# Forty-four of 1024 softmax score tiles take their exponential on VectorE and GpSimd instead of ScalarE

## The chip, the core and the metric

The kernel runs as one program on one core of a Trainium2 chip. The metric is device time in microseconds (us) of one execution. The kernel before was timed in three runs: 493.62, 494.31 and 499.47 us, median 494.31 us. One further execution was profiled; it took 492.96 us, and the span that the profile shows of it is 491.2 us.

Names of engines as in the profile: PE is TensorE, DVE is VectorE, ACT is ScalarE, POOL is GpSimd, SP issues DMAs. PSUM is the memory that PE writes to, in banks of 512 float32 per partition; SBUF is the working memory.

## The reference

The input is 2048 tokens of 448 numbers. Branch A is attention with 16 heads of 28, branch B a filter in the frequency domain; a sigmoid gate per token mixes them.

```
g = sigmoid((x * gate_w).sum(-1))
q, k, v = split(x @ wqkv)                 # 16 heads of 28
p = softmax(q @ k.T * 28 ** -0.5)         # 2048 x 2048 for each head
a = (p @ v) merged @ wo
b = irfft2(rfft2(x) * (w_r + 1j * w_i))
out = g * a + (1 - g) * b
```

The softmax has 16 x 2048 x 2048 = 67 million scores, and each needs an exponential. This is what the change is about.

## The kernel before, in words

**Tiles.** The scores are kept transposed: a score tile is 128 keys by 512 queries of one head, so one PSUM bank. Heads go in four groups T of four heads (`s` = 0 to 3, each on 32 rows of PE); queries go in four quarters q. A pair (T, q) is a chunk, and there are 16 chunks of 16 key blocks `i` by 4 heads, so 64 tiles each, 1024 in all.

**Steps.** `attention` (L554) cuts the row of 1024 tiles into steps of three (L558). Each step is one buffer `psS` of three PSUM banks, of which there are two (L158), and one exponential on ACT over all three banks, 128 x 1536, written as bf16 to `Pt` (`exps`, L582; six buffers `Pt`). That makes 341 ACT instructions of three tiles and one of one tile. The scale 28 ** -0.5 is given to it as an immediate, and so is a bias of zero. The queries were shifted beforehand by half norms (`nhk`), so that no maximum is needed.

**Order within step m** (L611 to L626): ACT's exponential of step m; PE's three score matmuls of step m+1 (`scores`, L565), with filler matmuls on a zero tile `warm` ahead of them where a count of PE's work says so (`filler`, L490); PE's value matmuls of eight finished tiles at a time (`values`, L591) into one PSUM bank `psPV`; then other work (`other_work`, L501); then whatever was put down in `later[m]`. A helper class (L113) keeps this order on every engine's queue: an engine runs its instructions in the order in which they were written, and one that waits holds up those behind it.

**Values.** `vsb` has a column of ones, so the sums of the softmax come out in `psPV` too. With a chunk's last tile, `normalise` (L671) puts down for later steps: a DVE transpose of `psPV` to `oU`, a reciprocal on DVE, a multiplication on POOL (`on`), and a DVE transpose to `oT` (which is `qT`). There is one `psPV` (L161), so the next chunk's first value matmul needs that first transpose done.

**Other work** is a list of units with due steps (`plan`, L438): keys and queries of later head groups (`k_units`, `q_units`), values, and the whole of branch B in matmuls (names `X`, `U`, `UT`, `Xri`, `G`, `V`, `VT`, `ZT`, `bm`). A unit is some PE matmuls into the one PSUM bank `bg` (L164), and then a DVE instruction that brings the bank to SBUF; the next unit can't write `bg` before. The budget of a step is `ROOM` = 1.22 us of PE time by a count of columns. POOL squares keys and queries (`sq`) for the half norms, multiplies in `normalise`, and does half of the complex product (`cm_t`, `G`).

**Ends.** `finish` (L629) does the last chunk's output. Before the first exponential, `head` (L243) transposes x and makes the first keys and queries. In it ACT runs some instructions with a bias read from SBUF (`keep`, L280, L284: `kT<-pk,kbt`) and some without (`sq<-pk`, L278).

Of the kernel before, what the change touches and what calls it, by code (L numbers as in the profile page):

```python
# [8 lines left out]

BF16 = mybir.dt.bfloat16  # L10
F32 = mybir.dt.float32
ACT = mybir.ActivationFunctionType
ALU = mybir.AluOpType
AX = mybir.AxisListType

P = 128
# [19 lines left out]
FEND = 318  # L36
BUSY = 1650
UNIT = 1000
F = D // 2 + 1
F2 = 2 * F  # L40
J = P // NT
# [94 lines left out]
class Kernel:  # L136
# [42 lines left out]
    def loads(self):  # L179
        nc, per = self.nc, self.per  # L180
        cc = self.consts = fft_consts()
        self.warm = per.tile([P, QW], BF16, name="warm")
        nc.vector.memset(self.warm[:], 0.0)
        c_IS = nc.inline_tensor(cc["IS"], name="cIS")
        self.IS = per.tile([P, 2 * P], BF16, name="IS")
        wqkv = self.A_wqkv.rearrange("(c p) (w n) -> p c w n", p=CK, w=3)
        self.W0 = per.tile([CK, NC_, 2, CK], BF16, name="W0")
        nc.sync.dma_start(out=self.W0[:, :, 1, :], in_=wqkv[:, :, 1, 0:CK])
        nc.scalar.dma_start(out=self.IS[:], in_=c_IS.ap())
        nc.scalar.dma_start(out=self.W0[:, :, 0, :], in_=wqkv[:, :, 0, 0:CK])  # L190
        self.ident = self.IS[:, 0:P]
        self.sel = self.IS[:, P:2 * P]
        self.xtok = [per.tile([P, 4, D], BF16, name=f"xtok{g}", tag=f"xb{g}") for g in range(4)]
        for g in range(4):
            nc.sync.dma_start(out=self.xtok[g][:], in_=self.x[:, 4 * g:4 * g + 4, :])
        self.kbt = per.tile([P, 1], F32, name="kbt")
        self.kb = self.kbt[:, 0:1]
        wv = self.A_wqkv[:, 2 * D:3 * D].rearrange("(c p) n -> p c n", p=CK)
        self.Wv = per.tile([CK, NC_, D + 1], BF16, name="Wv")
        nc.sync.dma_start(out=self.Wv[:, :, 1:D + 1], in_=wv)  # L200
        nc.sync.dma_start(out=self.Wv[:, :, 0:1],
                          in_=self.gate_w.rearrange("(c p o) -> p c o", p=CK, o=1))
        self.Wqk = per.tile([CK, NC_, 2 * D], BF16, name="Wqk")
        nc.sync.dma_start(out=self.Wqk[:],
                          in_=self.A_wqkv[:, 0:2 * D].rearrange("(c p) n -> p c n", p=CK))
        self.Bd = per.tile([CK, NC_, F2], BF16, name="Bd")
        nc.sync.dma_start(out=self.Bd[:], in_=nc.inline_tensor(cc["Bd"], name="cBd").ap())
        self.WqP = per.tile([CK, NC_, H, 32], BF16, name="WqP")
        self.WkP = per.tile([CK, NC_, H, 32], BF16, name="WkP")
        for Wp in (self.WkP, self.WqP):  # L210
            nc.gpsimd.memset(Wp[:, :, :, DH:32], 0.0)
        self.vsb = per.tile([P, NT, H, 32], BF16, name="vsb")
        nc.gpsimd.memset(self.vsb[:, :, :, DH:32], 0.0)
        nc.gpsimd.memset(self.vsb[:, :, :, DH:DH + 1], 1.0)
        self.wk = self.Wqk[:, :, D:2 * D].rearrange("p c (h d) -> p c h d", d=DH)
        self.wq = self.Wqk[:, :, 0:D].rearrange("p c (h d) -> p c h d", d=DH)
        self.xT = per.tile([CK, NC_, S], BF16, name="xT")
        self.qT = [per.tile([P, S], BF16, name=f"qT{T}") for T in range(NTH)]
        self.kT = [per.tile([P, S], BF16, name=f"kT{T}") for T in range(NTH)]
        self.oT = self.qT  # L220
        self.nm = [per.tile([P, NQ], F32, name=f"nm{T}") for T in range(NTH)]
        self.nhk = [per.tile([P, 1], F32, name=f"nhk{T}") for T in range(NTH)]
        self.glog = per.tile([P, NT], F32, name="glog")
        self.gsb = per.tile([P, NT], F32, name="gsb")
        self.omg = per.tile([P, NT], F32, name="omg")
        self.R = per.tile([P, 4, 256], BF16, name="R")
        self.Binv = per.tile([P, 2 * len(FCH), D], BF16, name="Binv")
        self.c_CS = nc.inline_tensor(cc["CS"], name="cCS")
        self.c_RB = nc.inline_tensor(cc["RB"], name="cRB")
        self.Wr_v = self.B_w_r.rearrange("(m g) f -> g m f", g=NT)  # L230
        self.Wi_v = self.B_w_i.rearrange("(m g) f -> g m f", g=NT)
        self.WoP = per.tile([P, NTH, D], BF16, name="WoP")
        nc.gpsimd.memset(self.WoP[:], 0.0)
# [128 lines left out]
    def q_units(self, T, g):  # L362
# [17 lines left out]
                                           op0=ALU.add, op1=ALU.add)  # L380
        return (("qa", T, g), a), (("q", T, g), b)

    def k_units(self, T, g):
        nc = self.nc
        st = {}

        def a():
            pk = self.ps_bg([P, QW], F32, name="pkb")
            yield from self.proj_mm(pk[:], self.WkP, T, g)
            kT = self.kT[T][:, QW * g:QW * g + QW]  # L390
            nc.vector.tensor_scalar(out=kT, in0=pk[:], scalar1=self.kb, scalar2=None,
                                    op0=ALU.add)
            sq = st["sq"] = self.rot3.tile([P, QW], BF16, name="sq")
            nc.gpsimd.tensor_tensor(out=sq[:], in0=kT, in1=kT, op=ALU.mult)
# [150 lines left out]
    def gate(self):  # L545
# [5 lines left out]
        nc.vector.tensor_scalar(out=self.omg[:], in0=self.gsb[:], scalar1=-1.0, scalar2=1.0,  # L551
                                op0=ALU.mult, op1=ALU.add)

    def attention(self):  # L554
        nc = self.nc
        chunks = [(T, q) for T in range(NTH) for q in range(NQ)]
        seq = [(ci, i, s) for ci in range(len(chunks)) for i in range(NT) for s in range(4)]
        steps = [seq[m:m + 3] for m in range(0, len(seq), 3)]  # L558
        n = len(steps)
        psS, Pt = {}, {}  # L560

        group = [len([1 for k in range(3 * m, 3 * m + 3) if k % GROUP == GROUP - 1])
                 for m in range(n + 1)]

        def scores(m):  # L565
            T, q = chunks[steps[m][-1][0]]
            self.need(("k", T, NQ - 1))
            self.need(("q", T, q))
            ps = psS[m] = self.ps_S([P, 3, QW], F32, name="psS")
            self.base = QW  # L570
            if m > 1:
                pv = GROUP // 4 * QW * group[m - 2]
                room = ROOM + ALLOW - self.over - 3 * SWITCH - QW * MM - pv * MM
                self.base += self.filler(m - 1, room, QW + pv, ps)
            for e, (ci, i, s) in enumerate(steps[m]):
                T, q = chunks[ci]
                nc.tensor.matmul(ps[:, e, :],
                                 lhsT=self.kT[T][32 * s:32 * s + 32, P * i:P * i + P],
                                 rhs=self.qT[T][32 * s:32 * s + 32, QW * q:QW * q + QW],
                                 start=True, stop=True, tile_position=(32 * s, 0))  # L580

        def exps(m):  # L582
            ne = len(steps[m])
            pt = Pt[m] = self.rotP.tile([P, 3, QW], BF16, name="Pt")
            nc.scalar.activation(out=pt[:, 0:ne, :], in_=psS.pop(m)[:, 0:ne, :], func=ACT.Exp,
                                 scale=SCALE)

        self.psPV = None
        pending = []

        def values(m, least):  # L591
            room = 0.0
            while len(pending) >= least:
                ci = pending[0][2][0]
                T, q = chunks[ci]
                for pt, e, (_, i, s) in pending[:least]:
                    self.need(("v", 1, i) if T else ("v", 0, i // 2))
                    if i == 0 and s == 0:
                        self.psPV = self.ps_pv([P, QW], F32, name="psPV")
                    nc.tensor.matmul(self.psPV[32 * s:32 * s + 32, :],  # L600
                                     lhsT=self.vsb[:, i, 4 * T + s, :], rhs=pt[:, e, :],
                                     start=(i == 0), stop=(i == NT - 1), tile_position=(0, 32 * s))
                del pending[:least]
                room += SWITCH + least / 4 * QW * MM
                self.base += least // 4 * QW
                if i == NT - 1 and s == 3:
                    self.normalise(m, T, q, self.psPV)
            return room

        scores(0)  # L610
        for m in range(n + 1):  # L611
            if m < n:
                exps(m)
            if m + 1 < n:
                scores(m + 1)
            if m > 0:
                pending += [(Pt[m - 1], e, x) for e, x in enumerate(steps[m - 1])]
            late = m >= n - 3
            fill = self.base - QW
            used = fill * MM + values(m, 4 if late else GROUP)  # L620
            used += 2 * SWITCH + QW * MM
            if m < n:
                used += self.other_work(m, ROOM + ALLOW - self.over - used, self.base)
            self.over = max(0.0, self.over + used - ROOM)
            for f in self.later.pop(m, []):
                f()  # L626
        assert not (self.current or self.units or self.later)
# [298 lines left out]
```

## Time and profile before

| what | value |
|---|---|
| three runs | 493.62, 494.31, 499.47 us; median 494.31 |
| the profiled execution | 492.96 us, span 491.2 us, mean granted PE clock 0.986 |
| busy: PE, DVE, ACT, POOL | 392.2, 195.5, 471.3, 85.5 us |
| first exponential starts, last three-tile one ends | 18.31 us, 480.73 us |
| DMA | 12.67 MB, mean 26 GB/s |

A row of the list of groups reads: line, engine, operation, written<-read, shapes, number of instructions, then busy time in us and mean ns of one, then the idle time of the engine just before them and what ended it. Nearly all rows have line L119, since a helper records every instruction; the names of the tiles tell them apart. Busy time is a union: where records of one engine overlap, the time is counted once, while the mean is of the whole records. A row of the timeline is start, length, engine, operation, tiles, shape and count, with the idle time before it in brackets; one row can hold several instructions in a row, and its length then runs from the first start to the last end. In the table of stretches, each row gives the length of the stretch and then each engine's busy time and number of instructions.

### The profile page before, as it was taken

To read this page: it belongs to the slowest core of one execution; us is meant where nothing else is said; L and a number is where in the kernel's file an instruction comes from. 1 tells how busy PE (TensorE), PEld (TensorE's weight loads), DVE (VectorE), ACT (ScalarE), POOL (GpSimd) and SP (SyncE) were. 2 spreads that over 40 slices of the span, in tenths; PEclk is the share of its full clock that TensorE was granted. 3 is DMA by queue.
4 is the path that set the end of the run, shared out by engine and by line. 5 is a ranking of instruction groups with operands and counts; after the bars stand their busy time and mean duration, and the time that the engine had idled before them with its cause. 6 is when DMAs were issued, how large, how long until landed. Compare 5 with 4: busy or idle time off the path is not lost.

```text
span 491.2 us, 7735 instructions
## 1 busy us (share of the span) xinstructions
PE 392.2 (80%) x3154; PEld 146.4 (30%) x3154; DVE 195.5 (40%) x338; ACT 471.3 (96%) x364; POOL 85.5 (17%) x125
## 2 busy tenths in 40 slices
PE   8877777779878887877777778778887778888876
PEld 5422222222222233332333223333233232323221
DVE  5421222322332344437566664443333333434413
ACT  5899999999999999998999999999999999999992
POOL 4100111040000111105455541101000000000000
PEclk9999999998999999998999999999999999999997
DMA  8800000000000000001122200000000000100001
GB/s 253 194 1 1 2 1 0 1 0 1 1 1 1 0 1 1 0 2 43 39 62 53 67 1 0 2 1 21 12 23 11 23 12 20 52 29 20 11 28 38
DMA packets 15515, 12.67 MB, mean 26 GB/s; under 512 B 6984, under 2 KB 14600, under 8 KB 15480
## 3 DMA queue, kind: packets, MB, share of 16 engines
q1 hardware_dynamic: 14728, 11.91, 9.0%
q8 instruction: 24, 0.39, 0.3%
q10 hardware_dynamic: 752, 0.28, 0.2%
q14 instruction: 11, 0.09, 0.1%
HBM read 10.35 MB, written 1.84 MB: 25 GB/s over the span
## 4 chain that ended last, share of the span: by engine, by line
ACT 57%; issue 21%; PE 16%; DVE 3%; DMA 1%; POOL 1%; DVEq 0%; SPq 0%; ACTq 0%; POOLq 0%
ACT Pt L119 57%; PE psS L119 5%; PE psPV L119 3%; PE pq L119 1%; PE pvp L119 1%; DMA xtok<-in_A_x_dram 1%; PE pt L119 1%; PE pwt L119 1%; PE pk L119 1%; PE psB L119 1%; DVE qT L119 0%; PE pkb L119 0%; DVE kT L119 0%; DVE qr L119 0%; POOL sq L119 0%
## 5 line engine op out<-in xcount | busy, mean ns | idle before, releaser
L119 ACT ACTIVATE Pt<-psS 128x1536 bf16<-128x1536 f32 x342 | 459.9, 1613 | 4.8 <-PE psS L119 4.6
L119 PE MATMUL psS<-qT,kT 32*128 32x512 bf16 x1024 | 134.8, 385 | 44.9 <-ACT Pt L119 41.6
L119 PEld LDWEIGHTS <-kT 32*128 32x128 bf16 x1024 | 42.5, 91 | 160.5 <-issue 156.2
L119 PE MATMUL psPV<-Pt,vsb 128*32 128x512 bf16 x1024 | 80.5, 390 | 1.2 <-DVE oU L119 1.2
L119 PE MATMUL psS<-warm 128*128 128x512 bf16 (+14 forms) x152 | 41.8, 332 | 21.4 <-ACT Pt L119 20.6
L119 POOL TENSOR_TENSOR sq<-qr 128x512 bf16<-128x512 bf16 x16 | 16.7, 1041 | 134.4 <-DVE qr L119 134.4
L119 POOL TENSOR_TENSOR sq<-kT 128x512 bf16<-128x512 bf16 x12 | 12.5, 1041 | 114.9 <-DVE kT L119 114.9
L119 POOL TENSOR_TENSOR on<-oU,rc 128x512 bf16<-128x512 f32 x15 | 15.7, 1048 | 90.5 <-DVE rc L119 90.5
L119 PEld LDWEIGHTS <-warm 128*128 128x128 bf16 x178 | 17.4, 101 | 36.6 <-issue 31.9
L119 POOL TENSOR_TENSOR cm_t<-Xri,Wg 128x225 bf16<-128x225 bf16 x32 | 20.3, 655 | 29.0 <-DVE Xri L119 29.0
L119 PEld LDWEIGHTS <-vsb 128*32 128x32 bf16 x1024 | 15.6, 94 | 30.9 <-issue 30.9
L119 DVE CAST vsb<-pvp 128x336 bf16<-128x336 f32 x16 | 8.1, 508 | 36.3 <-PE pvp L119 36.3
L119 DVE CAST X<-psx 128x450 bf16<-128x450 f32 x16 | 10.0, 627 | 30.4 <-PE psx L119 30.4
L119 DVE TENSOR_SCALAR bm<-psY,omg 128x448 bf16<-128x448 f32 x16 | 10.9, 684 | 24.4 <-PE psY L119 24.4
L119 DVE CAST qr<-pq 128x512 bf16<-128x512 f32 x16 | 11.1, 691 | 23.9 <-PE pq L119 23.9
L119 PEld LDWEIGHTS <-xT 112*128 112x128 bf16 x192 | 13.4, 97 | 22.2 <-issue 18.1
L119 PE MATMUL pq<-xT,WqP 112*128 112x512 bf16 x64 | 18.1, 381 | 1.8 <-DVE U L119 0.5
L119 DVE CAST ZT<-psZ 113x512 bf16<-113x512 f32 x16 | 11.1, 692 | 17.2 <-PE psZ L119 17.2
L119 PE MATMUL pf<-WoP,qT 128*128 128x448 bf16 x60 | 15.7, 355 | 2.2 <-DVE qT L119 0.8
L119 PE MATMUL psx<-Bd,xT 112*128 112x450 bf16 x64 | 16.5, 357 | 1.0 <-DVE kT L119 0.5
L119 DVE CAST U<-psA 113x512 bf16<-113x512 f32 x16 | 11.1, 692 | 15.3 <-PE psA L119 15.3
L119 DVE SCALAR_TENSOR_TENSOR fin<-pf,gsb,bm 128x448 bf16<-128x448 f32 x12 | 8.2, 684 | 21.7 <-PE pf L119 21.7
(82 smaller groups left out, 350.2 us busy)
## 6 DMA issues: line engine op xcount, KB each, us to landing
RBg<-cRB SPq DMA_DIRECT2D x16, 128.0 KB, 2.1
xtok<-in_A_x_dram SPq DMA_DIRECT2D x4, 448.0 KB, 4.7
out_dram<-fin SPq DMA_DIRECT2D x15, 112.0 KB, 1.7
CSg<-cCS SPq DMA_DIRECT2D x16, 96.0 KB, 1.9
Wg<-in_B_w_r_dram SPq DMA_DIRECT2D x16, 56.2 KB, 1.8
Wg<-in_B_w_i_dram SPq DMA_DIRECT2D x16, 56.2 KB, 1.9
Wqk<-in_A_wqkv_dram SPq DMA_DIRECT2D x1, 784.0 KB, 10.4
Binv<-cBinv SPq DMA_DIRECT2D x1, 448.0 KB, 13.7
```

The costliest lines, as they stand in the source:

```text
L119: return lambda *a, **k: self._tc.keep_in_program_order(f(*a, **k))
```

## The change

A few tiles of each chunk leave ACT. `AWAY` says at which steps after a chunk's start one tile is taken away: 0, 5 and 11 in fourteen chunks, 0 alone in chunks 7 and 8, so 44 tiles. Such a step still has three score tiles in its three banks, but ACT's exponential covers two of them, 128 x 1024. So ACT now has 297 exponentials of three tiles, 44 of two and one of one: 342, as before.

The third bank is read by DVE. With y = score * scale / ln 2 * 2^23 taken as an integer, the upper bits are the exponent of the result and the lower 23 a fraction; the result is the power of two times a polynomial of degree four in the fraction. Per tile (128 x 512) there are

- on DVE: `bits` from PSUM (multiply, maximum, to int32), in step m; `frac` (and, or) in step m+1; the power of two (and, xor, in place in `bits`) in m+2; three instructions `scalar_tensor_tensor` on float32 in m+5, m+6 and m+7, the last of which writes bf16 `px`;
- on POOL: an addition of a constant and a multiplication, both float32, in m+1.

The value matmul of such a tile comes `LAG` = 9 steps after its score. The leading coefficient is not multiplied in: instead every exponential on ACT now has a bias, log(2 / POLY[4]), read from a tile `shift` (128 x 1 in SBUF), where before the bias was an immediate zero. The budget of a step with a tile taken away is 0.4 us smaller (`SHORT`).

`kT` of groups 2 and 3 now takes the buffers of groups 0 and 1, and `Wqk` shares a buffer with `U` and `V` (tag `UV`). No DMA is added or moved. PE has the same 1024 score and 1024 value matmuls, and 158 fillers in `psS` instead of 152.

```
+BITS = SCALE / float(np.log(2.0)) * 2.0 ** 23
+LEAST = -126.0 * 2.0 ** 23
+ONE = 0x3F800000
+POLY = (37.67976179, 23.05395003, 12.31057451, -0.15702562, 0.01353417)
+AWAY = {c: [0, 5, 11] if c not in (7, 8) else [0] for c in range(16)}
+LAG = 9
+SHORT = 0.4
...
+        self.shift = per.tile([P, 1], F32, name="shift")
+        nc.vector.memset(self.shift[:], float(np.log(2.0 / POLY[4])))
...
-        self.Wqk = per.tile([CK, NC_, 2 * D], BF16, name="Wqk")
+        self.Wqk = per.tile([CK, NC_, 2 * D], BF16, name="Wqk", tag="UV")
...
+    def new_keys(self, T):
+        self.kT[T] = self.per.tile([P, S], BF16, name=f"kT{T}", tag=f"kT{T % 2}")
...
+    def away(self, m, score, turn):
+        nc = self.nc
+        bits = self.rot2.tile([P, QW], I32, name="bits")
+        frac = self.rot2.tile([P, QW], I32, name="frac")
+        h = self.rot2.tile([P, QW], F32, name="horner")
+        px = self.rot3.tile([P, QW], BF16, name="px")
+        read = nc.vector.tensor_scalar(out=bits[:], in0=score, scalar1=BITS, scalar2=LEAST,
+                                       op0=ALU.mult, op1=ALU.max)
...
+        def fraction():
+            nc.vector.tensor_scalar(out=frac[:], in0=bits[:], scalar1=0x7FFFFF, scalar2=ONE,
+                                    op0=ALU.bitwise_and, op1=ALU.bitwise_or)
+            nc.gpsimd.tensor_scalar(out=h[:], in0=x, scalar1=POLY[3], scalar2=None, op0=ALU.add)
+            nc.gpsimd.tensor_tensor(out=h[:], in0=h[:], in1=x, op=ALU.mult)
+
+        def power():
+            nc.vector.tensor_scalar(out=bits[:], in0=bits[:], scalar1=0x7F800000,
+                                    scalar2=0x40000000, op0=ALU.bitwise_and,
+                                    op1=ALU.bitwise_xor)
+
+        def times(c, by, out):
+            nc.vector.scalar_tensor_tensor(out=out[:], in0=h[:], scalar=c, in1=by,
+                                           op0=ALU.add, op1=ALU.mult)
+        for d, f in ((1, fraction), (2, power), (5, lambda: times(POLY[2], x, h)),
+                     (6, lambda: times(POLY[1], x, h)),
+                     (7, lambda: times(POLY[0], bits[:].bitcast(F32), px))):
+            self.later.setdefault(m + d, []).append(f)
+        return px
...
         def exps(m):
-            ne = len(steps[m])
-            pt = Pt[m] = self.rotP.tile([P, 3, QW], BF16, name="Pt")
-            nc.scalar.activation(out=pt[:, 0:ne, :], in_=psS.pop(m)[:, 0:ne, :], func=ACT.Exp,
-                                 scale=SCALE)
+            acts, away = steps[m]
+            ne = len(acts)
+            ps = psS.pop(m)
+            pt = self.rotP.tile([P, 3, QW], BF16, name="Pt")
+            turn = nc.scalar.activation(out=pt[:, 0:ne, :], in_=ps[:, 0:ne, :], func=ACT.Exp,
+                                        scale=SCALE, bias=self.shift[:, 0:1])
+            ready.setdefault(m + 1, []).extend((pt[:, e, :], x) for e, x in enumerate(acts))
+            for x in away:
+                px = self.away(m, ps[:, ne, :], turn)
+                ready.setdefault(m + LAG, []).append((px[:], x))
...
+            self.room = ROOM
             if m < n:
+                self.room -= SHORT * len(steps[m][1])
                 exps(m)
```

More of the change, by code (lines that the diff above doesn't have):

```diff
@@ L11 @@
 F32 = mybir.dt.float32
+I32 = mybir.dt.int32
 ACT = mybir.ActivationFunctionType
@@ L218, in loads @@
         self.qT = [per.tile([P, S], BF16, name=f"qT{T}") for T in range(NTH)]
-        self.kT = [per.tile([P, S], BF16, name=f"kT{T}") for T in range(NTH)]
+        self.kT = {}
+        self.new_keys(0)
         self.oT = self.qT
@@ L387, in a @@
         def a():
+            if g == 0:
+                self.new_keys(T)
             pk = self.ps_bg([P, QW], F32, name="pkb")
@@ L552, in gate, with steps @@
                                 op0=ALU.mult, op1=ALU.add)
+    def steps(self, chunks):
+        away, acts = {}, []
+        for ci in range(len(chunks)):
+            away[ci] = [(o, (ci, 4 * k, k)) for k, o in enumerate(AWAY.get(ci, []))]
+            out = [x for _, x in away[ci]]
+            acts += [(ci, i, s) for i in range(NT) for s in range(4) if (ci, i, s) not in out]
+        steps, first = [], {}
+        while acts:
+            ci = acts[0][0]
+            m = len(steps)
+            first.setdefault(ci, m)
+            off = [away[ci].pop(0)[1]] if away[ci] and away[ci][0][0] <= m - first[ci] else []
+            k = 3 - len(off)
+            steps.append((acts[:k], off))
+            del acts[:k]
+        assert not any(away.values())
+        return steps
@@ new lines, in away @@
+    def away(self, m, score, turn):
[6 more added lines that the diff above has]
+                                       op0=ALU.mult, op1=ALU.max)
+        self.tc.declare_no_dep(read.ins, turn.ins, reason="another bank")
+        x = frac[:].bitcast(F32)
+        def fraction():
[15 more added lines that the diff above has]
+        return px
@@ L556, in attention @@
         chunks = [(T, q) for T in range(NTH) for q in range(NQ)]
-        seq = [(ci, i, s) for ci in range(len(chunks)) for i in range(NT) for s in range(4)]
-        steps = [seq[m:m + 3] for m in range(0, len(seq), 3)]
+        steps = self.steps(chunks)
         n = len(steps)
-        psS, Pt = {}, {}
-        group = [len([1 for k in range(3 * m, 3 * m + 3) if k % GROUP == GROUP - 1])
-                 for m in range(n + 1)]
+        psS, ready = {}, {}
+        ends = [0]
+        for m in range(n + 1):
+            new = len(steps[m - 1][0]) if m else 0
+            new += sum(1 for k in (m - LAG,) if k >= 0 and steps[k][1])
+            ends.append(ends[-1] + new)
+        group = [ends[m + 1] // GROUP - ends[m] // GROUP for m in range(n + 1)]
         def scores(m):
-            T, q = chunks[steps[m][-1][0]]
+            tiles = steps[m][0] + steps[m][1]
+            T, q = chunks[tiles[len(steps[m][0]) - 1][0]]
             self.need(("k", T, NQ - 1))
@@ L571, in scores @@
             if m > 1:
-                pv = GROUP // 4 * QW * group[m - 2]
-                room = ROOM + ALLOW - self.over - 3 * SWITCH - QW * MM - pv * MM
+                pv = GROUP // 4 * QW * group[m - 1]
+                room = self.room + ALLOW - self.over - 3 * SWITCH - QW * MM - pv * MM
                 self.base += self.filler(m - 1, room, QW + pv, ps)
-            for e, (ci, i, s) in enumerate(steps[m]):
+            for e, (ci, i, s) in enumerate(tiles):
                 T, q = chunks[ci]
@@ L582, in exps @@
         def exps(m):
-            ne = len(steps[m])
-            pt = Pt[m] = self.rotP.tile([P, 3, QW], BF16, name="Pt")
-            nc.scalar.activation(out=pt[:, 0:ne, :], in_=psS.pop(m)[:, 0:ne, :], func=ACT.Exp,
-                                 scale=SCALE)
+            acts, away = steps[m]
[8 more added lines that the diff above has]
+                ready.setdefault(m + LAG, []).append((px[:], x))
         self.psPV = None
         pending = []
+        count = [0] * 4
         def values(m, least):
@@ L593, in values @@
             while len(pending) >= least:
-                ci = pending[0][2][0]
-                T, q = chunks[ci]
-                for pt, e, (_, i, s) in pending[:least]:
+                for ap, (ci, i, s) in pending[:least]:
+                    T, q = chunks[ci]
                     self.need(("v", 1, i) if T else ("v", 0, i // 2))
-                    if i == 0 and s == 0:
+                    if not any(count):
                         self.psPV = self.ps_pv([P, QW], F32, name="psPV")
                     nc.tensor.matmul(self.psPV[32 * s:32 * s + 32, :],
-                                     lhsT=self.vsb[:, i, 4 * T + s, :], rhs=pt[:, e, :],
-                                     start=(i == 0), stop=(i == NT - 1), tile_position=(0, 32 * s))
+                                     lhsT=self.vsb[:, i, 4 * T + s, :], rhs=ap,
+                                     start=(count[s] == 0), stop=(count[s] == NT - 1),
+                                     tile_position=(0, 32 * s))
+                    count[s] += 1
                 del pending[:least]
@@ L605, in values @@
                 self.base += least // 4 * QW
-                if i == NT - 1 and s == 3:
+                if min(count) == NT:
+                    count[:] = [0] * 4
                     self.normalise(m, T, q, self.psPV)
             return room
+        self.room = ROOM
         scores(0)
         for m in range(n + 1):
+            self.room = ROOM
             if m < n:
+                self.room -= SHORT * len(steps[m][1])
                 exps(m)
@@ L615, in attention @@
                 scores(m + 1)
-            if m > 0:
-                pending += [(Pt[m - 1], e, x) for e, x in enumerate(steps[m - 1])]
+            pending += ready.pop(m, [])
             late = m >= n - 3
@@ L622, in attention @@
             if m < n:
-                used += self.other_work(m, ROOM + ALLOW - self.over - used, self.base)
-            self.over = max(0.0, self.over + used - ROOM)
+                used += self.other_work(m, self.room + ALLOW - self.over - used, self.base)
+            self.over = max(0.0, self.over + used - self.room)
             for f in self.later.pop(m, []):
```

## The prediction

> **What bounds the kernel now.** I read the page first for who is busy, then the groups, then the timeline of ACT in the head for the one thing that the change does to every exponential, then a stall, then a table of stretches.
>
> The page: ACT is busy 96% of the span, and the chain that ended last lies on its exponentials.
>
> ```profile
> span 491.2 us, 7735 instructions
> PE 392.2 (80%) x3154; PEld 146.4 (30%) x3154; DVE 195.5 (40%) x338; ACT 471.3 (96%) x364; POOL 85.5 (17%) x125
> ...
> ACT 57%; issue 21%; PE 16%; DVE 3%; DMA 1%; POOL 1%; DVEq 0%; SPq 0%; ACTq 0%; POOLq 0%
> ```
>
> The groups. The 342 exponentials make 459.9 us of the 491.2, with only 4.8 us of idle time before them: ACT sets the time. Their records overlap (342 x 1613 ns would be 552 us), so the price of one is not 1613 ns but busy time over count: the first starts at 18.31 us and the 341st ends at 480.73, so 462.4 us less 4.8 idle, over 341, is 1.342 us. The other rows give prices for the added work.
>
> ```profile
> L119 ACT ACTIVATE Pt<-psS 128x1536 bf16<-128x1536 f32 x342 | 459.9, 1613 | 4.8 <-PE psS L119 4.6
> ...
> L119 POOL TENSOR_TENSOR on<-oU,rc 128x512 bf16<-128x512 f32 x15 | 15.7, 1048 | 90.5 <-DVE rc L119 90.5
> ...
> L119 DVE SCALAR_TENSOR_TENSOR qT<-pq,nhk,qr 128x512 bf16<-128x512 f32 x15 | 11.2, 749 | 10.7 <-PE pq L119 10.7
> ...
> L119 DVE TENSOR_SCALAR kT<-pkb,kbt 128x512 bf16<-128x512 f32 x12 | 9.0, 747 | 16.2 <-PE pkb L119 16.2
> ...
> L119 ACT ACTIVATE sq<-pk 128x512 bf16<-128x512 f32 x4 | 2.4, 600 | 1.3 <-PE pk L119 1.3
> ...
> L119 ACT ACTIVATE kT<-pk,kbt 128x512 bf16<-128x512 f32 x3 | 1.9, 685 | 0.0
> ```
>
> ACT's timeline at the end gives the price per element: 128x1536 alone takes 1.45 us, 128x512 alone 0.60 us, so 1024 elements are 0.85 us and one tile is 0.427 us.
>
> ```profile
> 479.28 1.45 ACT L119 ACTIVATE Pt<-psS 128x1536 bf16<-128x1536 f32 x1
> 481.38 0.60 ACT L119 ACTIVATE Pt<-psS 128x512 bf16<-128x512 f32 x1 [0.65 <-PE psS L119]
> ```
>
> ACT's timeline in the head shows what a bias read from SBUF costs. `sq` has an immediate bias, `kT` a bias from the tile `kbt`; both read 128x512 from PSUM.
>
> ```profile
> 11.77 0.60 ACT L119 ACTIVATE sq<-pk 128x512 bf16<-128x512 f32 x1 [0.94 <-PE pk L119]
> 12.27 0.68 ACT L119 ACTIVATE kT<-pk,kbt 128x512 bf16<-128x512 f32 x1
> 12.84 1.01 ACT L119 COPY xT<-pt 112x1024 bf16<-112x1024 bf16 x1
> ...
> 14.68 0.60 ACT L119 ACTIVATE sq<-pk 128x512 bf16<-128x512 f32 x1 [0.33 <-PE pk L119]
> 15.17 1.26 ACT L119 ACTIVATE kT<-pk,kbt 128x512 bf16<-128x512 f32 x2
> ```
>
> From `sq` to the next start is 0.50 us (11.77 to 12.27) and 0.49 (14.68 to 15.17). From `kT` to the next start is 0.57 (12.27 to 12.84), and two `kT` back to back last 1.26 us, which is 0.68 and a pitch of 0.58. No idle time lies between them. So the bias from SBUF adds 0.07 to 0.09 us to what an instruction holds the engine, even where the next one is already there.
>
> A stall, and the load of DVE by stretch:
>
> ```profile
> 224.89 0.70 DVE L119 STREAM_TRANSPOSE oU<-psPV 128x512 f32<-128x512 f32 x1
> ...
> 225.65 0.83 PE L119 MATMUL psPV<-Pt,vsb 128*32 128x512 bf16 x8 [1.18 <-DVE oU L119]
> ...
> 227.55 1.45 ACT L119 ACTIVATE Pt<-psS 128x1536 bf16<-128x1536 f32 x1 [0.84 <-PE psS L119]
> ```
>
> ```profile
> 220.00:249.00 29.00, 22.63 (x197) 8.73 (x197) 18.18 (x36) 27.52 (x21) 13.37 (x20) 0.94 0.17 41
> 249.00:278.00 29.00, 21.77 (x208) 8.77 (x208) 19.21 (x37) 29.00 (x23) 15.21 (x23) 1.00 0.28 69
> 278.00:336.00 58.00, 45.99 (x382) 18.92 (x380) 28.84 (x46) 57.38 (x44) 13.80 (x17) 1.00 0.01 2
> ```
>
> The stall shows how DVE, which bounds nothing, reaches ACT: DVE came late to the transpose of `psPV`, PE waited 1.18 us, and ACT then 0.84 us for scores. But DVE at 66% (249 to 278: 19.21 of 29.00) stalls ACT not at all.
>
> **The change, part by part.**
>
> *Fewer elements on ACT.* 44 tiles x 0.427 us = -18.8 us, all on the path. The number of exponentials stays 342, so no fixed cost goes.
>
> *A bias from SBUF in every exponential.* The trace has no exponential with one; it has `kT`. Bounds: 0, if it hides behind the overlap of the long records, and 0.09 us, from the two `kT` back to back (0.58 less 0.49). I take 0.076, from the unrounded starts of those same rows (494 and 570 ns), since `kT` held its successor up by it with no idle time between. 341 x 0.076 = +25.9 us (0 to +30.7). A rule speaks on this: the Trainium skill, "ScalarE: Activation LUTs", section "What ACT_TABLE_LOAD costs", says that each pointer operand of one value per partition adds about 93 ns to an instruction, beside 186 ns and 0.833 ns per element, and that neighbours overlap by about 93 ns. By that figure the term would be 341 x 0.093 = +31.7 us, an estimate from that page, and the change slower still; the rows decide, and I keep theirs.
>
> These two give +7.1 us for a stream of exponentials that never waits.
>
> *The score buffer is held by DVE too.* Scores of step m+2 need both ACT's exponential and DVE's `bits` of step m done. A two-tile exponential takes 1.342 + 0.076 - 0.427 = 0.99 us from the end of the one before. `bits` costs 0.75 (the row of `kT` on DVE, also 128x512 from PSUM). It is queued on DVE behind whatever brought `bg` home for step m-1, and in 14 of the 44 places behind a polynomial instruction of the tile before. With DVE free it ends 0.8 after the exponential's start, so nothing is lost; behind a full 0.75 us instruction it ends at 1.56, 0.57 late. Behind the wait on PE stand value matmuls and other work, and ACT two steps on. Scores took 0.39 us and were ready a median 0.59 us before ACT needed them (their ends against the ends of the exponentials), which covers most of it. Bounds: 0 to 44 x 0.57 = 25 us; I take +1.5, nearer to nothing because of that lead.
>
> *The polynomial on DVE and POOL.* On DVE 0.75 for `bits`, 3 x 0.75 (row `qT<-pq`), and two bit operations between 0.24 (the reciprocal on 16 elements, a fixed cost) and 0.75: I take 0.5, together 4.0 us a tile, 176 us in all. DVE goes from 195.5 to 371 us, some 74%. On POOL two operations of at most 1.05 (row `on`): 92 us on top of 85.5. No element of that is on the path by itself: of the nine steps to the value matmul, seven are taken, and the 2.1 us on POOL have four steps (5.6 us). For the bit operations, which read float-sized integers in SBUF, "VectorE: DVE Perf Modes", "The perf-mode tier table", gives two elements a cycle; with that page's 58 cycles of fixed cost and 0.96 GHz it would be 0.33 us each, an estimate from the page that no row here shows, and DVE's load some 15 us smaller.
>
> What it costs is that evacuations come later. From 278 to 336 six tiles bring DVE from 28.84 to 53 us of 58; from 220 to 278 only two are added, 78%. There `psPV`'s transpose and `bg` wait longer, and PE with them. Against that, 297 steps are 76 ns longer, which is PE's to spend. Bounds: -4 us, if the longer steps remove nearly all of the 4.8 us of idle time, and +12, if each stretch of 29 us stalls like 220 to 249 (1.5 us for half of the 16 chunks). I take +3.
>
> *At nothing:* squares `sq` and `on` get up to 2.1 us of POOL ahead of them; POOL is 17% busy, and the matmul that needs `sq` comes a unit later (if that cover went, 27 x 1 us). `kT` of groups 2 and 3 is first written at 166.7 and 283.7 us, and its new buffer was last read when chunks 3 and 7 ended, about 133 and 250 us. `U` is written from 176 us on, `Wqk` was last copied at 103 us. SP's and POOL's DMA queues are not touched. The memset of `shift` is one small DVE instruction in the head. Six more fillers: PE waits for ACT anyway. Tail (480.7 to 491.2) and head (18.3) stay.
>
> Sum: -18.8 + 25.9 + 1.5 + 3 = +11.6 us. On the profiled execution (492.96, span 491.2) that is 504.6, span 502.8; the median of the runs lies 1.35 above that execution, and against it 494.31 + 11.6 = 505.9. I say 505.5.
>
> **The rivals.**
>
> 1. *The bias hides* (faster). Exponentials are dispatched while the one before is still in flight: mean record 1.61 for a pitch of 1.34, so 0.27 us ahead, three times what the bias costs. If it is fetched in that time, the term is 0: 494.31 - 18.8 + 4.5 = 480. Break-even is 18.8 / 341 = 55 ns per exponential, 42 ns with the waits. Against it: `kT` was followed without a gap too, overlapped its successor by 0.11 us, and still held it by the full 0.076.
> 2. *The bias costs, and the waits do not come* (within 2%). The longer steps give PE more room, DVE's added load is off the path: 494.31 + 7.1 - 2 = 499. For it: the stretch at 66% DVE without a stall.
> 3. *DVE becomes the local bound* (slower by far). DVE at 91% from 278 to 336, and `bits` holding the score buffers in all places: +7.1 and 12 to 25 of stalls, 513 to 526, say 520. Against it: 74% on the whole, and nine steps of patience.
>
> **How the numbers follow.** Chances: forecast (bias in full, stalls of 3 to 12 us) 0.55, 501.5 to 512; rival 1 0.08; rival 2 0.22, 495 to 501.5; rival 3 0.15. The range takes rival 2 whole and the lower part of rival 3: 495 to 517. Slower by over 2%, which is about what a measurement of this kernel can tell from no change, is above 504.2: 0.37 of the forecast's 0.55 and rival 3, 0.52. Within 2%: the rest of the forecast and rival 2, 0.40. Faster by over 2%: 0.08.
>
> **What would show it.** In the profile after, three-tile exponentials at a pitch of 1.42 us confirm the bias, at 1.34 refute it; two-tile ones at 0.99 or 0.92. ACT's idle time before `Pt` should be 8 to 12 us; over 15 is rival 3. `bits<-psS` near 0.75 us, DVE busy near 371 us, and waits of `psS` for DVE `bits` few and short. It is wrong if the bias is free, or if DVE's queue makes PE wait at most of the 44 places.

## The result, and the profile after

The changed kernel took 541.0 us in the median of four runs (536.4 to 547.4); the kernel before 494.4. The ratio is 1.089, with a 95% interval of 1.077 to 1.101; it is one of means and leaves out the run of 547.4 us, which fell in a slower state, while the medians here and below are of all runs. The profiled execution took 539.06 us, its span is 537.3 us (491.2 before).

The page of the changed kernel: its first line, the busy times, and the chain of waits. ACT is still the busiest, but in a longer span, and PE, DVE and POOL now hold 61% of the chain, where it was 20%.

```profile
span 537.3 us, 8096 instructions
PE 423.2 (79%) x3160; PEld 150.6 (28%) x3160; DVE 350.1 (65%) x603; ACT 488.4 (91%) x364; POOL 218.0 (41%) x213
...
PE 30%; ACT 26%; DVE 22%; issue 13%; POOL 9%; DVEq 0%; ACTq 0%; POOLq 0%
```

The groups of the changed kernel: the exponential, and POOL's two operations for a tile taken away. The idle time before the exponentials went from 4.8 us to 34.7. POOL needs 1.52 and 1.32 us, where the prediction had at most 1.05 each.

```profile
L127 ACT ACTIVATE Pt<-psS,shift 128x1536 bf16<-128x1536 f32 (+1 forms) x342 | 477.0, 1508 | 34.7 <-PE psS L127 33.9
...
L127 POOL TENSOR_SCALAR horner<-frac 128x512 f32<-128x512 f32 x44 | 66.9, 1521 | 193.7 <-DVE frac L127 193.7
...
L127 POOL TENSOR_TENSOR horner<-horner,frac 128x512 f32<-128x512 f32 x44 | 57.9, 1315 | 3.7
```

ACT's timeline in a stretch without waits gives the new pitch: seven exponentials in 10.14 us, one of them alone 1.54, so (10.14 - 1.54) / 6 = 1.433 us.

```profile
336.26 10.14 ACT L127 ACTIVATE Pt<-psS,shift 128x1536 bf16<-128x1536 f32 x7
```

The list of waits of the changed kernel (who waited for whom: us in all, times, longest):

```profile
PEld L127 <- DVE bits L127: 42.7, 39, 3.9
ACT Pt L127 <- PE psS L127: 33.9, 41, 4.0
...
PE psS L127 <- DVE bits L127: 21.5, 20, 3.7
...
DVE qT L127 <- POOL on L127: 20.1, 13, 3.7
```

PE's weight loads wait for `bits` 39 times; there are 44 such places. And DVE waits 20.1 us for POOL's `on`. The same line of the kernel before:

```profile
DVE qT L119 <- POOL on L119: 4.8, 4, 2.0
```

To add the waits up for every kernel in the same way, I take from each trace the ends of successive exponentials. Their distance in undisturbed steps is the pitch of the form, and its sum over all steps is the "stream"; what is longer than the pitch is "waits". (The idle time in the row above is a little smaller, because an exponential that starts late has no record in front of it to overlap with.) Before: pitch 1.342, stream 456.3, waits 4.7. After: pitch 1.431 and 1.004, stream 468.2, waits 40.8. So 11.9 us of the 46 came from the stream and 36.1 from waits; a rest of some -2 us lies at the first and last exponential and in the tail. Every stream and every wait below is read from one profiled execution of its kernel, while the times of one kernel spread by up to 11 us, so differences of a few us are not firm.

**Where the waits come from.** The timeline of the changed kernel around step 5 of chunk 1 shows the main case (chunks and their steps count from 0). The rows of PE's weight loads and some others are left out.

```profile
52.60 5.49 ACT L127 ACTIVATE Pt<-psS,shift 128x1536 bf16<-128x1536 f32 x4
...
53.68 1.66 POOL L127 TENSOR_SCALAR horner<-frac 128x512 f32<-128x512 f32 x1
...
55.42 1.27 POOL L127 TENSOR_TENSOR horner<-horner,frac 128x512 f32<-128x512 f32 x1
...
56.65 1.05 POOL L127 TENSOR_TENSOR on<-oU,rc 128x512 bf16<-128x512 f32 x1
57.73 0.71 DVE L127 STREAM_TRANSPOSE qT<-on 128x512 bf16<-128x512 bf16 x1 [3.74 <-POOL on L127]
58.36 0.47 DVE L127 CAST vsb<-pvp 128x336 bf16<-128x336 f32 x1
58.76 0.68 DVE L127 TENSOR_SCALAR bits<-psS 128x512 int32<-128x512 f32 x1
...
59.49 0.57 PE L127 MATMUL psS<-warm 128*128 128x512 bf16 x2 [2.84 <-DVE bits L127]
...
60.71 1.54 ACT L127 ACTIVATE Pt<-psS,shift 128x1536 bf16<-128x1536 f32 x1 [2.62 <-PE psS L127]
```

Read it from the bottom. ACT waits 2.62 us for scores; PE could not write them, since DVE had not yet read the tile of the buffer's last use (`bits`); `bits` stood behind an evacuation and the transpose `qT<-on`; and that stood still at the head of DVE's queue for 3.74 us, since POOL did the two operations of the polynomial (53.68 to 56.69) before `on`.

The longest wait has another cause. It lies in chunk 9, where the complex product of branch B fills DVE and POOL:

```profile
316.00 2.33 DVE L127 TENSOR_TENSOR cm_t<-Xri,Wg 128x225 bf16<-128x225 bf16 x2
...
318.36 0.99 DVE L127 TENSOR_TENSOR G<-cm_t,cm_t 128x225 bf16<-128x225 bf16 x1
...
319.27 0.70 DVE L127 STREAM_TRANSPOSE qT<-on 128x512 bf16<-128x512 bf16 x1
319.90 0.65 DVE L127 TENSOR_SCALAR bits<-psS 128x512 int32<-128x512 f32 x1
...
320.60 0.91 PE L127 MATMUL psS<-warm 128*128 128x512 bf16 x2 [3.69 <-DVE bits L127]
...
322.16 3.06 ACT L127 ACTIVATE Pt<-psS,shift 128x1536 bf16<-128x1536 f32 x2 [3.96 <-PE psS L127]
```

From 312 to 321 us DVE is busy for 8.73 of 9.00 us, and `qT` does not wait for POOL: `bits` is late because of the work ahead of it. The `cm_t` and `G` shown take 3.35 us together, where the same three instructions took 1.45 at 312.09. Chunk 9 has 8.2 of the 40.8 us of waits, the most of any chunk.

What came after the stall at 56.6 us is a second loss. The table of stretches from there on (columns: length, busy times of PE, its weight loads, DVE, ACT and POOL, then the granted PE clock):

```profile
56.50:59.50 3.00, 0.16 (x5) 0.01 (x1) 1.77 (x4) 1.59 (x2) 1.20 (x2) 1.00 0.00 0
59.50:63.00 3.50, 3.50 (x15) 0.70 (x15) 2.90 (x5) 2.29 (x2) 1.82 (x1) 0.56 0.00 0
63.00:66.00 3.00, 2.70 (x17) 0.59 (x17) 0.75 (x1) 2.47 (x3) 1.33 (x3) 0.50 0.00 0
66.00:69.00 3.00, 2.94 (x10) 0.96 (x10) 0.51 (x1) 2.41 (x2) 1.02 (x1) 0.50 0.00 0
69.00:72.00 3.00, 2.95 (x16) 0.49 (x14) 2.27 (x4) 1.54 (x1) 1.42 (x1) 0.50 0.00 0
```

PE stood still for nearly 3 us, and then its clock was granted at half for 13.7 us, with PE busy nearly all of that time and ACT waiting for it. In the whole span the clock was at half for 65 us (14 before). Exponentials that start in those stretches have 24.5 of the 40.8 us of waits; that includes the direct waits for `bits` at 60.71 and 322.16 us, so it is not the clock's share alone.

### The profile page after: what moved, and what is told of

Its sections match the earlier page's. It is cut to its first block, busy times and chain, and to the rows that moved or that the text cites. A ratio compares the mean times of both kernels' runs of the same rounds, so it can differ in the third digit from the quotient of the medians.

```text
span 537.3 us, 8096 instructions
## 1 busy us (share of the span) xinstructions
PE 423.2 (79%) x3160; PEld 150.6 (28%) x3160; DVE 350.1 (65%) x603; ACT 488.4 (91%) x364; POOL 218.0 (41%) x213
## 4 chain that ended last, share of the span: by engine, by line
PE 30%; ACT 26%; DVE 22%; issue 13%; POOL 9%; DVEq 0%; ACTq 0%; POOLq 0%
ACT Pt L127 26%; PE psS L127 9%; POOL horner L127 6%; PE psPV L127 5%; DVE bits L127 3%; PE pq L127 3%; DVE qT L127 3%; POOL on L127 2%; PE psx L127 2%; DVE cm_t L127 2%; DVE horner L127 2%; PE pkb L127 1%; PE psA L127 1%; PE pf L127 1%; DVE Xri L127 1%
## 5 line engine op out<-in xcount | busy, mean ns | idle before, releaser
L127 ACT ACTIVATE Pt<-psS,shift 128x1536 bf16<-128x1536 f32 (+1 forms) x342 | 477.0, 1508 | 34.7 <-PE psS L127 33.9
L127 POOL TENSOR_SCALAR horner<-frac 128x512 f32<-128x512 f32 x44 | 66.9, 1521 | 193.7 <-DVE frac L127 193.7
L127 PE MATMUL psPV<-Pt,vsb 128*32 128x512 bf16 x980 | 90.8, 408 | 0.2 <-ACT Pt L127 0.2
L127 PE MATMUL psS<-warm 128*128 128x512 bf16 (+20 forms) x158 | 45.1, 338 | 33.1 <-ACT Pt L127 16.0
L127 DVE SCALAR_TENSOR_TENSOR horner<-horner,frac 128x512 f32<-128x512 f32 x88 | 62.5, 710 | 3.5 <-POOL horner L127 2.8
L127 POOL TENSOR_TENSOR horner<-horner,frac 128x512 f32<-128x512 f32 x44 | 57.9, 1315 | 3.7
L127 DVE SCALAR_TENSOR_TENSOR px<-horner,bits 128x512 bf16<-128x512 f32 x44 | 31.8, 724 | 0.3
L127 DVE TENSOR_SCALAR bits<-psS 128x512 int32<-128x512 f32 x44 | 29.9, 679 | 1.6 <-PE psS L127 1.5
L127 DVE TENSOR_SCALAR bits<-bits 128x512 int32<-128x512 int32 x44 | 29.6, 672 | 0.0
L127 DVE STREAM_TRANSPOSE qT<-on 128x512 bf16<-128x512 bf16 x15 | 10.6, 710 | 20.1 <-POOL on L127 20.1
L127 PE MATMUL pq<-xT,WqP 112*128 112x512 bf16 x64 | 20.1, 418 | 4.6 <-DVE V L127 1.4
L127 DVE CAST qr<-pq 128x512 bf16<-128x512 f32 x16 | 11.0, 690 | 18.8 <-PE pq L127 18.8
L127 PEld LDWEIGHTS <-xT 112*128 112x128 bf16 x192 | 13.7, 100 | 25.4 <-issue 21.4
```

Of the source, the lines that this page charges most:

```text
L127: return lambda *a, **k: self._tc.keep_in_program_order(f(*a, **k))
```

## The experiments

My theory after reading this: the bias costs 30 us, and the waits come from DVE's queue, through the wait for POOL and the held score buffer. The rival: DVE (65% busy) is simply too full. The kernel before was timed again beside each group of kernels, with medians of 493.5 to 494.4 us; the ratios go by those. The edits below are shortened to the words that change.

| kernel | median us | ratio to before (95%) | stream | waits | PE clock |
|---|---|---|---|---|---|
| changed | 541.0 | 1.089 (1.077 to 1.101) | 468.2 | 40.8 | 0.940 |
| e1, before + bias | 526.9 | 1.067 (1.063 to 1.070) | 485.9 | 9.7 | 0.964 |
| e2, changed, no bias | 530.4 | 1.070 (1.063 to 1.077) | 437.6 | 62.9 | 0.929 |
| e3, changed, POOL later | 516.0 | 1.043 (1.038 to 1.047) | 468.2 | 17.5 | 0.977 |
| e4, changed, no hold | 546.0 | 1.105 (1.101 to 1.109) | 486.5 | 26.6 | 0.931 |
| e5 = e2 + e3 | 498.8 | 1.010 (1.007 to 1.014) | 438.0 | 29.9 | 0.988 |
| e6 = e3 + early read | 509.1 | 1.033 (1.027 to 1.040) | 467.8 | 9.5 | 0.985 |
| e7 = e6, no bias | 490.9 | 0.993 (0.990 to 0.996) | 438.0 | 22.7 | 0.985 |
| e8 = e4 + POOL later | 533.8 | 1.082 (1.076 to 1.087) | 486.2 | 15.5 | 0.948 |
| e9 = e7, 39 tiles | 481.8 | 0.977 (0.974 to 0.979) | 440.1 | 11.2 | 1.000 |

**e1: the bias alone.**

```
-func=ACT.Exp, scale=SCALE)
+func=ACT.Exp, scale=SCALE, bias=self.shift[:, 0:1])     # the kernel before; shift = 0
```

> The kernel before, with a bias of zero read from SBUF in every exponential and nothing else. Theory A (the bias costs what the pitch of the changed kernel shows, 1431 less 1342 ns, 89 ns for each of 341): +30 us, so 524 to 525 us, less up to 3 us of idle time that longer steps hide: 521 to 525. Theory B (the longer pitch has another cause, such as DVE reading PSUM beside ACT): 494 to 500 us.

526.9 us. The stream is 29.6 us longer, 87 ns for each of 341. The waits did not shrink with the longer steps, as I had thought, but grew by 5 us; PE's clock was at half for 38 us in place of 14, and 5.1 of the 9.7 us lie there. PE waits longer for ACT (85.9 us in all, 62.3 before): each of the ten stretches at half follows 3.4 us in which PE was busy only 57 to 65%, with no single wait over 1.04 us. Theory A, 2 us over its range, with that addition.

The groups of e1, for comparison with the row of before (459.9 us busy, 4.8 idle):

```profile
L119 ACT ACTIVATE Pt<-psS,shift 128x1536 bf16<-128x1536 f32 x342 | 490.6, 1678 | 8.1 <-PE psS L119 8.0
```

**e2: the changed kernel without the bias.**

```
-scalar2=LEAST, op0=ALU.mult, op1=ALU.max)               # LEAST = -126 * 2 ** 23
+scalar2=OFFSET, op0=ALU.mult, op1=ALU.add)              # log2(POLY[4] / 2) * 2 ** 23
-func=ACT.Exp, scale=SCALE, bias=self.shift[:, 0:1])
+func=ACT.Exp, scale=SCALE)
```

> The changed kernel without the bias: the constant goes into the bits by an added offset in place of the lower limit (which these scores never reach), the exponential has an immediate bias again. Theory A (bias 30 us, waits independent of it): 541 - 30 = 511 us, with ACT idle before the exponentials near 35 us. Theory B (the shorter steps leave PE and DVE less time, and the waits grow by what the bias gave them): 520 to 535 us, idle time 45 to 60 us.

530.4 us: the stream fell by 30.6 us, and the waits rose by 22.1. Theory B: while the waits stand, most of the bias's price is hidden in them. The list of waits of e2:

```profile
ACT Pt L127 <- PE psS L127: 51.6, 63, 4.1
...
PEld L127 <- DVE bits L127: 47.0, 39, 4.1
...
DVE qT L127 <- POOL on L127: 20.9, 13, 3.7
```

**e3: POOL's two operations one step later**, behind `on` in POOL's queue.

```
-for d, f in ((1, fraction), (2, power), ...             # fraction: DVE's frac and POOL's two
+for d, f in ((1, fraction), (2, pool), (2, power), ...  # fraction: frac alone
```

> The changed kernel with POOL's two operations one step later (m+2 in place of m+1), so that the multiplication of the softmax normalisation goes ahead of them and DVE's transpose of it does not wait. Same work. Theory A (that wait at the head of DVE's queue holds the score buffer of the tile taken at step 5, and the slow PE clock after it makes the waits at step 11): waits fall by 15 to 30 us, 511 to 526 us, and DVE's wait for POOL's product falls from 20 us to under 6. Theory B (DVE is too full on the whole): 536 to 541 us.

516.0 us, 25 less with the same work, and DVE's wait for `on` is nearly gone. DVE's busy time is the same (346.4 us), so these 25 us were not its load. Theory A.

```profile
PEld L127 <- DVE bits L127: 30.8, 35, 2.3
...
ACT Pt L127 <- PE psS L127: 13.7, 24, 1.6
...
DVE qT L127 <- POOL on L127: 1.9, 2, 0.9
```

**e4 and e8: the load without the hold.** ACT does all tiles; DVE and POOL do the polynomial on a constant tile, and its result is not used. In e8 POOL's part is a step later too.

```
-read = nc.vector.tensor_scalar(out=bits[:], in0=score, ...
+nc.vector.tensor_scalar(out=bits[:], in0=self.fake[:], ...
-turn = nc.scalar.activation(out=pt[:, 0:ne, :], ...
+turn = nc.scalar.activation(out=pt[:, 0:na, :], ...     # na = 3
-ready.setdefault(m + LAG, []).append((px[:], x))
+ready.setdefault(m + 1, []).append((pt[:, ne, :], x))
```

> The changed kernel with all of the polynomial's work on DVE and POOL, but on a constant tile in SBUF whose result is not used; ACT does all three tiles of every step, with the bias. So DVE's load stays (less some 0.3 us a tile, since the first read is from SBUF) and no score buffer is held by DVE. Stream of exponentials 341 x 1.431 = 488 us, 20 more than in the changed kernel. Theory A (the held score buffer makes the waits): idle time falls from 41 us in all to 5 to 12, 525 to 533 us. Theory B (DVE's load delays the other work, and PE with it): waits stay above 30 us, 550 us or more.

e4 took 546.0 us with 26.6 us of waits: between the two theories. The hold is not the only way: DVE's wait for POOL costs time without it too, as e8 shows. The way is probably the other work, whose bank `bg` comes home late; no run shows that by itself.

```profile
DVE qT L127 <- POOL on L127: 26.3, 12, 3.7
ACT Pt L127 <- PE psS L127: 22.6, 33, 2.2
```

> The kernel with the unused polynomial on a constant tile (no score buffer held, ACT does all tiles, with the bias), and POOL's operations a step later: DVE's and POOL's load alone, without either of the two waits. Theory A (load alone costs little): waits fall from 26.6 us to the 10 us of the kernel with the bias alone, 526 to 531 us. Theory B (the load itself delays PE): waits stay above 20 us, 540 us or more.

e8 took 533.8 us, with 15.5 us of waits, 12.1 of them while the clock was at half. That is over the 526 to 531 that I gave, and under theory B. Against e1, which has the same stream and none of the load (9.7), the load of the polynomial costs 5.8 us by the waits and 7 by the medians; the runs of e8 spread over 6 us.

**e5: both.** The edits of e2 and e3.

> Immediate bias and POOL's operations a step later, together. Stream of exponentials 437.6 us, as measured without the bias. Theory A (what the bias takes away from the waits is lost again whatever the waits' cause: +22 us as between the changed kernel and the one without bias): waits 17.5 + 22 = 40 us, 504 to 508 us. Theory B (waits grow in proportion, 62.9 to 40.8 times 17.5 = 27 us): 491 to 495 us.

498.8 us with waits of 29.9: nearer to theory B (27) than to A (40). With the wait for POOL gone, taking the bias off gains 17 us; with it, it gained 11.

**e6: DVE's read put directly behind its score matmuls**, one step earlier in DVE's queue and so ahead of that step's evacuations.

```
+            if steps[m][1]:                              # at the end of scores(m)
+                taken[m] = self.take(ps[:, len(steps[m][0]), :])
```

> POOL's operations a step later, bias as in the changed kernel, and DVE's read of the score tile put directly behind its score matmuls (one step earlier in DVE's queue, ahead of the other work's evacuations of that step), so that the score buffer is free by the end of the exponential. Theory A (what is left of the waits, 17.5 us, is the held score buffer): waits fall to the 8 to 10 us of the kernel with the bias alone, 506 to 509 us, and PE's weight loads wait for bits under 5 us in place of 31. Theory B (what is left is DVE's load): 514 to 517 us.

509.1 us; waits 9.5, the same sum as with the bias alone (9.7). Theory A: most of what was left was the held buffer. That the two sums agree is in part luck, though, as the waits lie elsewhere: chunks 7 and 9 have 7.8 of the 9.5 us here and 2.0 of the 9.7 in e1. In chunk 9 `bits` is still 2.0 us late behind DVE's other work, and PE waits 2.02 us for it.

```profile
ACT Pt L127 <- PE psS L127: 7.8, 9, 2.2
PEld L127 <- DVE bits L127: 3.5, 4, 2.3
```

**e7: all three.** The edits of e2, e3 and e6.

> Immediate bias, POOL's operations a step later, and DVE's read of the score tile directly behind its matmuls. Stream 437.6 us. Theory A (with no held buffer and no wait for POOL, the waits stay under 20 us): 475 to 487 us, faster than the kernel before. Theory B (steps without the bias leave PE and DVE too little time): waits of 30 us or more, 497 us or above.

490.9 us, between the two ranges, and 0.7% faster than before, a difference clear of its interval but small. The short steps do have waits (22.7 us in place of 9.5), and 12.4 of them lie in chunks 7 to 9.

**e9: no tile taken in chunks 7, 8 and 9**, where the complex product fills POOL and DVE.

```
-AWAY = {c: [0, 5, 11] if c not in (7, 8) else [0] for c in range(16)}
+AWAY = {c: [0, 5, 11] if c not in (7, 8, 9) else [] for c in range(16)}
```

> The fastest version so far (immediate bias, POOL later, early read), with no tile taken away in chunks 7, 8 and 9, where POOL and DVE are full with the complex product: 39 tiles in place of 44. In that version chunks 7 to 9 wait 3.3, 2.5 and 6.6 us and gain 5 x 0.427 = 2.1 us. Theory A (their waits come from the tiles taken away there): 12.4 us of waits fall to the 2.5 us of the kernel before in these chunks, less 2.1 of gain: 8 us, 483 us. Theory B (these chunks wait for another reason, such as steps that are too short after a backlog): 489 to 493 us.

481.8 us against 494.0, 2.3% faster than before (theory A had 483), and PE's clock was never at half in the span. The waits of chunks 7 to 9 went from 12.4 us to 0.7; the rest did not move. The page and the exponential's row of e9:

```profile
span 479.3 us, 8056 instructions
PE 393.5 (82%) x3155; PEld 147.7 (31%) x3157; DVE 331.9 (69%) x573; ACT 457.4 (95%) x364; POOL 200.8 (42%) x203
```

```profile
L127 ACT ACTIVATE Pt<-psS 128x1536 bf16<-128x1536 f32 (+1 forms) x342 | 446.0, 1474 | 7.9 <-PE psS L127 7.0
```

DVE is busier here (69%) than in the changed kernel (65%), and the waits are about a quarter. With e3, where the same load waits 23.3 us less, that refutes the rival for the span as a whole: what stands in DVE's queue counts for more than its share of busy time. It does not refute it for chunk 9. There DVE is full, and moving POOL's part and reading early left 6.0 us of waits (e6). Taking the tiles away there removed nearly all of them.

## Why the prediction was right or wrong, point by point

- **ACT's elements: right.** -18.8 us; e2's stream against that of before is 437.6 - 456.3 = -18.7.
- **The bias: right, a little small.** 0.076 us was taken, 87 ns measured (29.6 us in place of 25.9). The upper bound, 0.09 from the two `kT` back to back, was nearer than the starts. The Trainium skill, "ScalarE: Activation LUTs", section "What ACT_TABLE_LOAD costs", has about 93 ns: the starts of the exponentials do move from 1.330 to 1.423 us, but the ends, which count, by 87 to 89 ns. The first rival, that the bias hides, is refuted.
- **At nothing, "squares `sq` and `on` get up to 2.1 us of POOL ahead of them": this is the step that failed.** For `sq` a cover was named, for `on` none. There was none: behind the transpose that waits for `on` stands all of DVE's queue, `bits` with it. POOL's 2.1 us were 2.8 besides. Moving POOL's part took 23.3 us of waits away (e3), what the half clock had added to them included.
- **The held score buffer: +1.5 us predicted, wrong.** I asked what DVE would be doing before `bits` and counted instructions at work, at most one of 0.75 us, so 0.57 late; that left out the time in which an instruction ahead of `bits` waits itself. The ends of `bits` against those of the exponential of the same step in the trace: at a chunk's step 0 on average 0.04 us late, at step 5 1.28 (up to 3.77), at step 11 1.23 (up to 2.72). At step 5 the transpose waits for POOL in 12 of 14 places; the 3.77 is in chunk 9, where it does not wait and DVE is full. Step 11 has a copy that waits for PE and a polynomial instruction; its two latest, 2.63 and 2.72, fall while PE is at half clock. POOL's part moved later brings step 5 down to 0.21 (e3), and the early read brings the averages of all three steps below zero (e6). With the early read, 8.0 us of waits went (e3 to e6). The lead of 0.59 us that was set against the term does not come out of the trace as described: the scores end a median 0.84 us before the end of the exponential ahead, and 0.50 before the start of their own.
- **DVE's load: +3 predicted; not settled.** e8 less e1 is 5.8 us, e6 less e1 is -0.2. What is clear is chunk 9: 8.2 us of waits in the changed kernel, 0.7 in e9 without its tiles. The sum spread the load over the stretches and priced it as late evacuations; it cost most in one chunk, through `bits`. DVE's busy time was 350 us (371 predicted): `bits` 0.68, the polynomial's 0.71, the bit operations 0.45 and 0.67.
- **PE's half clock was not in the sum.** 24.5 of the 40.8 us of waits belong to exponentials that start while it lasted. It follows on PE's waits in the trace, and is gone in e9; its own share was not measured apart, since no run held the clock up with the waits left in.
- **Longer steps as room for PE** (-4 us, at best): wrong in sign for the kernel before, where the bias alone (e1) made the waits 5 us longer, half of all at the half clock. But with the tiles taken away the longer steps do cover waits: without the bias they are 22.1 us longer in the changed kernel (e2), 12.4 in e3 (e5) and 13.2 in e6 (e7). So with the tiles taken away, removing the bias gained 11 to 18 us by the medians, not the 29.6 of the stream.
- **The third rival** named the mechanism nearest to the outcome (`bits` holding the buffers), but priced it at 12 to 25 us and laid it to DVE's load. The direction of the forecast was right; its waits, +4.5 us, were an eighth of the 36.1 measured, and its stream, +7.1, came out at +11.9. A slip in the chances besides: stalls of 3 to 12 us on 494.31 + 7.1 are 504.4 to 513.4, not 501.5 to 512.

Some things stay open: why e8 has more waits (15.5) than e6 (9.5), where the load is the same and the steps shorter, beyond that 12.1 of them fall at half clock; and what causes e9's last 11.2 us, which are spread over the chunks, with at most 2.0 in one.

## What to carry to other kernels

Before work is added to an engine that is off the path, look in its queue for instructions that wait for a third engine: everything behind them inherits that wait, and a buffer that the new work holds carries it onto the path. Put the instruction that frees a shared buffer directly behind its producer, and new work behind the old in every queue where the old has someone waiting. And count operand forms, not only elements: a bias from SBUF in 341 instructions cost ACT more (29.6 us) than the elements taken away had gained (18.7). And look at the load by stretch: DVE's mean of 65% hid 9 us in which it was full.

## What the runs showed of the hardware

- After a 2.84 us wait PE's clock was granted at half for 13.7 us, though PE was busy nearly throughout; other stretches at half lasted as little as 3.4 us. All are multiples of 3.41 us, but for those that the end of a trace cuts off. Cut the eleven traces into pieces of that length, in step with the changes, without the first 19 and last 12 us of each. PE's busy share in the piece ahead was 71% or less at each of the 63 changes to half, and 93% or more at each of the 62 changes back. All 18 pieces under 50% at full clock were followed by half clock, none of the 1136 over 71%; between, either happened. The Trainium skill, "TensorE: Matmul & The Clock Gate", section "What's actually happening", has an idle window of about 3.4 us for the way down and a busy one of about 3.4 us for the way up. The length agrees. But the window need not be idle: many short waits were enough.
- On POOL, float32 with one input and a constant took 1.49 us for 128x512 (median), longer than the two-input product of float32 (1.27), or of bf16 before (1.04). The Trainium skill, "GPSIMD Engine Reference", section "4.1 Engine selection", calls one input "roughly line-rate" where it compares POOL with DVE; DVE's `bits`, also one input with constants, took 0.68.
- DVE's bit operations on int32 in SBUF took 0.38 us at best, but up to 1.52. The 40 in the changed kernel that no POOL instruction overlapped took at most 0.42; in the timeline at 52.89 us one lasts 1.10 us beside POOL's square and sum. That POOL's work slows them is likely by this, but which of its instructions do so was not tried.
